# Retention scores in half-height tiles and an undecayed state in one PSUM bank, ahead of two expert MLPs

## The chip, the cores and the metric

One core of a Trainium2 chip runs the whole program. The metric is device time in microseconds (us) from the start to the end of one execution. The core's engines run side by side and meet at semaphores: PE (TensorE, matrix products into PSUM), ACT (ScalarE), DVE (VectorE), POOL (GpSimd) and SP (which issues DMAs). Each engine executes its own list of instructions in order.

## The reference, cut to what matters

```python
# q, k, v: (2 batches, 8 heads, 768 tokens, 64)
gamma = 1.0 - 2.0 ** (-5.0 - np.arange(H))
state = np.zeros((B, H, D, D))
for t in range(S):
    state = gamma * state + np.einsum('bhd,bhe->bhde', k[:, :, t], v[:, :, t])
    y[:, :, t] = scale * np.einsum('bhd,bhde->bhe', q[:, :, t], state)
x = y.transpose(0, 2, 1, 3).reshape(1536, 512)
# then a top-1 mixture of 8 experts (512 -> 1024 -> 512, relu), and
# relu(x @ w_in) ** 2 @ w_out with 512 -> 2048 -> 512
```

Only the first part, the retention, is touched by the change. Every head has its own decay gamma.

## The kernel before, in words

The 1536 tokens are 12 chunks of 128 (six per batch, `NC = 6`). The recurrence is done by chunks. With keys scaled by a falling and queries by a rising power of gamma, the output of a chunk is a masked product inside the chunk (scores, then scores times values) plus the queries times the state that the earlier chunks left. Products of this part are in f32, and PE records two MATMULs for each of them.

Eight heads of 64 lie as four pairs (`NP = 4`) of 128 rows. The functions for chunk i are:

- `khat`, `qhat` (L351, L355): scale K and Q on POOL, 128x512 each. `ktrans`, `qtrans` (L364, L372) transpose them on PE and copy them out of PSUM on ACT.
- `ktrans` (L364) writes the transposed keys into `kpads`, where each head has 128 rows and the other head's 64 rows are zeros set once at the start (L301 to L304). Two ACT copies of 64x512 do that.
- `scores` (L390): for each of eight heads one product of the padded keys (128 rows) with the pair's queries (L396), then two masked copies on DVE (L397).
- `outer` (L402): keys times values of a pair, 128x128, of which only the two diagonal 64x64 blocks belong to the state (L410). DVE adds the former state (L414; ACT copies instead in a batch's first chunk, L416), and POOL multiplies with `g128` (L418), which holds gamma to the 128th on the diagonal blocks and zeros elsewhere. The result `tf` serves `attend` of the next chunk.
- `attend` (L421): queries times `tf` (L430, four full products), then scores times values (L433, eight products of 64 output rows, two heads side by side in the halves of the columns), all into one bank.
- `halve`, `gate`, `probs`, `weigh`, `natural`, `count`, `rank`, `spread`, `enter` (L437 to L525) split the output into two f16 parts (`xlo` on DVE), compute the router, and build the table of tokens by expert.

The order is written out by hand (`manual_schedule`). The loop at L573 does for i = 0 to 10:

```python
attend(i); enter(i - 1); halve(i); scores(i + 1); gate(i); natural(i)
probs(i); count(i); outer(i + 1); weigh(i); ktrans(i + 2); qtrans(...)
qhat(...); rank(i); spread(i); khat(i + 3)
```

From i = 3 on (`L - PRE`) each iteration also splits half a block of expert weights: the high part on ACT after `halve`, the low part (`w1lo` or `w2lo`, L149) on DVE at the end of the iteration. `outer` returns at once for a batch's last chunk, so iteration 4 has no `outer`. Loads of K, Q and V run four chunks ahead on SP's queue. After the loop come the experts (to about 246 us) and the dense MLP.

Of the kernel before, what the change touches and what calls it, by code (L numbers as in the profile page):

```python
# [9 lines left out]
F32 = mybir.dt.float32  # L10
F16 = mybir.dt.float16
I32 = mybir.dt.int32
AF = mybir.ActivationFunctionType
ALU = mybir.AluOpType
# [5 lines left out]
P = 128  # L20
# [7 lines left out]
def layout_consts(B, H, S, D, E, cap, widths):  # L28

    gamma = 1.0 - 2.0 ** (-5.0 - np.arange(H, dtype=np.float64))  # L30
    t = np.arange(P, dtype=np.float64)
    cols = {}
    cols["ident"] = np.eye(P)

    tq = (2 * t[:, None, None] + np.arange(2)[None, None, :]) % P
    cols["gk"] = gamma[None, :] ** ((P - 1) - t[:, None]) * 256.0
    cols["gq"] = (gamma[None, :, None] ** (tq - (P - 1)) * 4.0).reshape(P, -1)
    cols["mask"] = (t[:, None] <= t[None, :]).astype(np.float64)
    cols["tail"] = np.zeros((P, 0))
    cols["w2e"] = np.tile(2.0 ** -np.arange(E), (P, 1))  # L40
    n_tile = B * S // P
    cols["tok"] = t[:, None] + P * np.arange(n_tile)[None, :]
    cols["tok1"] = cols["tok"] + 1
    cols["wide"] = np.tile(np.array(widths), (P, 1))
    arr = np.concatenate([cols[c] for c in cols], axis=1).astype(np.float32)
    where, o = {}, 0
    for c in cols:
# [13 lines left out]
def kernel(  # L61
# [19 lines left out]
    PE, ACT, DVE, POOL = nc.tensor, nc.scalar, nc.vector, nc.gpsimd  # L81
    B, H, S, D = q.shape
# [11 lines left out]
    NP = H // 2  # L94
    NC = S // P
# [19 lines left out]
    def C(n, i=None):  # L115
        o, w = where[n]
        src, o = (c32t, o - last) if o >= last else (c32, o)
        return src[:, o:o + w] if i is None else src[:, o + i:o + i + 1]
# [171 lines left out]
    sb = actx.enter_context(tc.tile_pool(name="sb", bufs=2))  # L290
    ld = actx.enter_context(tc.tile_pool(name="ld", bufs=5))
    ps = ctx.enter_context(tc.tile_pool(name="ps", bufs=1, space=PSUM))
# [5 lines left out]
    table_up = sb.tile([P, 1], F32, name="table_up", bufs=1)  # L298
    DVE.memset(table_up, 0.0)
    ACT.activation(out=table_up, in_=table_up, func=AF.Copy)  # L300
    kpads = []  # L301
    for i in range(2):
        kpads.append(sb.tile([P, NP, 2, P], F32, name=f"kpad{i}", bufs=1))
        POOL.memset(kpads[i], 0.0)  # L304
    g128 = sb.tile([P, NP, P], F32, name="g128", bufs=1)
    POOL.memset(g128, 0.0)
    for h in range(H):
        r = slice(h % 2 * D, (h % 2 + 1) * D)
        POOL.memset(g128[r, h // 2, r], float((1.0 - 2.0 ** (-5.0 - h)) ** P))
    wg = sb.tile([P, KD, E], F32, name="wg", bufs=1)  # L310
    wghi = sb.tile([P, KD, E], F16, name="wghi", bufs=1)
    wglo = sb.tile([P, KD, E], F16, name="wglo", bufs=1)
# [21 lines left out]
    Q, K, V = {}, {}, {}  # L334
# [11 lines left out]
                store[i] = ld.tile([P, H, D], F32, name=nm, tag=nm)  # L346
                nc.sync.dma_start(store[i], src[b, :, c * P:(c + 1) * P, :].rearrange("h t d -> t h d"))

    QH, KH, QT, SC, A = {}, {}, {}, {}, {}

    def khat(i, eng=POOL):  # L351
        KH[i] = sb.tile([P, H, D], F32, name="kh", tag="kh", bufs=3)
        eng.tensor_tensor(KH[i], K.pop(i), C("gk").unsqueeze(2).to_broadcast([P, H, D]), op=ALU.mult)

    def qhat(u, r, eng=POOL):  # L355
        if 2 * u >= NT:
            return
        QH[u, r] = sb.tile([P, H, D], F32, name="qh", tag="qh")
        eng.tensor_tensor(QH[u, r], Q[u][:, :, r, :],
                           C("gq").rearrange("p (h r) -> p h r", r=2)[:, :, r:r + 1].to_broadcast([P, H, D]), op=ALU.mult)  # L360
        if r == 1:
            Q.pop(u)

    def ktrans(i):  # L364
        tk = ps.tile([P, NP, P], F32, name="tk", tag="tk")
        for p in range(NP):
            PE.transpose(tk[:, p, :], KH[i][:, 2 * p:2 * p + 2, :].rearrange("t h d -> t (h d)"), C("ident"))
        for j in range(2):
            r = slice(j * D, (j + 1) * D)
            ACT.activation(out=kpads[i % 2][r, :, j, :], in_=tk[r], func=AF.Copy)  # L370

    def qtrans(u, r, tag="tq", eng=ACT):  # L372
        if 2 * u >= NT:
# [13 lines left out]
    def queries(i):  # L387
        return QT[i // 2][:, :, i % 2].rearrange("p n i r -> p n (i r)")

    def scores(i):  # L390
        A[i] = sb.tile([P, H, P], F32, name="A", tag="A")
        for u in range(2):
            sc = ps.tile([P, H // 2, P], F32, name="sc", tag=f"sc{u}")
            for h in range(u * H // 2, (u + 1) * H // 2):
                p, j = divmod(h, 2)
                PE.matmul(sc[:, h % (H // 2), :], lhsT=kpads[i % 2][:, p, j, :], rhs=queries(i)[:, p, :], start=True, stop=True)  # L396
            DVE.tensor_tensor(A[i][:, u * H // 2:(u + 1) * H // 2, :], sc, C("mask").unsqueeze(1).to_broadcast([P, H // 2, P]), op=ALU.mult)  # L397

    TF, XO = {}, {}
    XT = {}  # L400

    def outer(i):  # L402

        b, c = divmod(i, NC)
        if c == NC - 1:
            return
        pp = ps.tile([P, NP, P], F32, name="pp", tag="pp")
        kh = KH[i]
        for p in range(NP):
            PE.matmul(pp[:, p, :], lhsT=kh[:, 2 * p:2 * p + 2, :].rearrange("t h d -> t (h d)"),  # L410
                      rhs=V[i][:, 2 * p:2 * p + 2, :].rearrange("t h d -> t (h d)"), start=True, stop=True)
        t0 = sb.tile([P, NP, P], F32, name="t0", tag="t0")
        if c:
            DVE.tensor_tensor(t0, pp, TF[i], op=ALU.add)  # L414
        else:
            ACT.activation(out=t0, in_=pp, func=AF.Copy)  # L416
        tf = sb.tile([P, NP, P], F32, name="tf", tag="tf")
        POOL.tensor_tensor(tf, t0, g128, op=ALU.mult)  # L418
        TF[i + 1] = tf

    def attend(i):  # L421
        b, c = divmod(i, NC)
        xo = ps.tile([P, NP, P], F32, name="xo", tag="xo")
        qt = queries(i)
        a = A.pop(i)
        vv = V[i]

        if c:
            for p in range(NP):
                PE.matmul(xo[:, p, :], lhsT=TF[i][:, p, :], rhs=qt[:, p, :], start=(p == 0), stop=False, skip_group_check=True)  # L430
        for p in range(NP):
            for j in range(2):
                PE.matmul(xo[j * D:(j + 1) * D, p, :], lhsT=vv[:, 2 * p + j, :], rhs=a[:, 2 * p + j, :],  # L433
                          start=(c == 0 and p == 0), stop=(p == NP - 1), skip_group_check=True)
        XO[i] = xo

# [196 lines left out]
    for s_ in range(2):  # L633
        for kk in range(KD):
            for g, (off, n) in zip(g0, blocks(0)):
                n = min(n, widths[0] - off)
                PE.matmul(xb[s_][kk // 2][:, kk % 2, off:off + n], lhsT=g[0:n, s_ * DM + kk * P:s_ * DM + (kk + 1) * P],
                          rhs=C16("ident")[0:n, 0:n], start=False, stop=False, skip_group_check=True)
# [598 lines left out]
```

## Time and profile before

| | us |
|---|---|
| median of 3 runs (range) | 498.01 (497.55 to 499.4) |
| the profiled execution: its own time | 498.74 |
| its span in the profile | 497.0 |
| PE busy in the span | 473.5 (95%) |
| DVE busy | 333.0 (67%) |
| ACT busy | 272.2 (55%) |
| POOL busy | 102.8 (21%) |
| mean granted TensorE clock, share of full | 0.994 |

The profiled execution took 1.7 us more than its span: that much lies around the instructions. PE is the busiest engine over the whole program, but the three parts of the program (retention to about 92 us, experts to about 246 us, dense MLP to the end) need to be read apart. A matmul's record lasts longer than its turn, because matmuls overlap in the array: starts and sums of rows tell more than the mean length of one.

### The profile page before, as it was taken

To read this page: it belongs to the slowest core of one execution; us is meant where nothing else is said; L and a number is where in the kernel's file an instruction comes from. 1 tells how busy PE (TensorE), PEld (TensorE's weight loads), DVE (VectorE), ACT (ScalarE), POOL (GpSimd) and SP (SyncE) were. 2 spreads that over 40 slices of the span, in tenths; PEclk is the share of its full clock that TensorE was granted. 3 is DMA by queue.
4 is the path that set the end of the run, shared out by engine and by line. 5 is a ranking of instruction groups with operands and counts; after the bars stand their busy time and mean duration, and the time that the engine had idled before them with its cause. 6 is when DMAs were issued, how large, how long until landed. Compare 5 with 4: busy or idle time off the path is not lost.

```text
span 497.0 us, 9864 instructions
## 1 busy us (share of the span) xinstructions
PE 473.5 (95%) x4069; PEld 363.0 (73%) x4069; DVE 333.0 (67%) x573; ACT 272.2 (55%) x396; POOL 102.8 (21%) x120
## 2 busy tenths in 40 slices
PE   7999999888989999999999999999999999999991
PEld 4898899888989999899944444444458884447881
DVE  3778999897968889787789998406773114675110
ACT  3567675676665767672356655519882007884000
POOL 4755564291032431400000000011000110000100
PEclk9999999999999999999999999999999999999997
DMA  9998894599698898896452200011000100000100
GB/s 207 253 287 238 236 312 136 159 332 338 130 335 227 280 363 277 258 355 228 152 184 90 87 0 1 0 44 43 1 1 1 44 22 21 1 0 1 44 21 29
DMA packets 56120, 71.30 MB, mean 143 GB/s; under 512 B 30705, under 2 KB 37233, under 8 KB 55042
## 3 DMA queue, kind: packets, MB, share of 16 engines
q1 hardware_dynamic: 53410, 63.77, 42.0%
q0 software_dynamic: 2512, 6.73, 4.1%
q8 instruction: 34, 0.56, 0.5%
q14 instruction: 20, 0.16, 0.1%
q10 hardware_dynamic: 144, 0.08, 0.1%
HBM read 63.73 MB, written 6.84 MB: 142 GB/s over the span
## 4 chain that ended last, share of the span: by engine, by line
PE 77%; DMA 8%; DVE 5%; issue 3%; POOL 3%; ACT 2%; SPq 0%; POOLq 0%; ACTq 0%; DVEq 0%
PE w L1078 14%; PE zp L905 8%; PE zp L904 8%; PE zp L906 8%; DMA rawi<-in_moe_w_in_dram 4%; PE sc L396 4%; PE yp L728 3%; PE op L929 3%; PE op L930 3%; PE op L928 3%; PE yp L729 3%; PE yp L727 3%; PE hp L711 3%; PE hp L713 3%; PE hp L712 3%
## 5 line engine op out<-in xcount | busy, mean ns | idle before, releaser
L905 PE MATMUL zp<-ylo,winhi 128*128 128x512 f16 x192 | 72.8, 379 | 0.0
L904 PE MATMUL zp<-yhi,winhi 128*128 128x512 f16 x192 | 72.8, 379 | 0.0
L906 PE MATMUL zp<-yhi,winlo 128*128 128x512 f16 x192 | 72.8, 379 | 0.0
L728 PE MATMUL yp<-hl,w2hi 128*128 128x232 f16 (+5 forms) x256 | 65.4, 255 | 3.4 <-DVE hl L717 3.4
L919 POOL DMA_INDIRECT out_dram<-ob,tid x12 | 11.8, 982 | 264.6 <-DVE ob L1099 124.6
L727 PE MATMUL yp<-hh,w2hi 128*128 128x232 f16 (+5 forms) x256 | 65.4, 255 | 0.0
L729 PE MATMUL yp<-hh,w2lo 128*128 128x232 f16 (+5 forms) x256 | 65.4, 255 | 0.0
L1078 PE MATMUL w<-WH,AH 128*128 128x256 f16 x224 | 61.0, 273 | 0.5 <-ACT ob L1093 0.5
L1078 PE MATMUL w<-WH,AL 128*128 128x256 f16 x224 | 61.1, 273 | 0.0
L1078 PE MATMUL w<-WL,AH 128*128 128x256 f16 x224 | 61.0, 273 | 0.0
L711 PE MATMUL hp<-xg,w1hi 128*128 128x192 f16 (+5 forms) x224 | 57.0, 255 | 0.0
L713 PE MATMUL hp<-xg,w1lo 128*128 128x192 f16 (+5 forms) x224 | 57.0, 254 | 0.0
L712 PE MATMUL hp<-xg,w1hi 128*128 128x192 f16 (+5 forms) x224 | 57.0, 254 | 0.0
L1078 PEld LDWEIGHTS <-AH 128*128 128x128 f16 x448 | 43.8, 98 | 6.3 <-issue 0.9
L149 DVE SCALAR_TENSOR_TENSOR w2lo<-raw,w2hi 128x1024 f16<-128x1024 f32 x32 | 40.6, 1270 | 7.7 <-ACT w2hi L146 7.6
L1046 DVE TENSOR_TENSOR AL<-x,AH 128x768 f16<-128x768 f32 (+1 forms) x32 | 34.8, 1087 | 14.4 <-ACT AH L1044 14.4
L149 DVE SCALAR_TENSOR_TENSOR w1lo<-raw,w1hi 128x1024 f16<-128x1024 f32 x32 | 42.0, 1321 | 0.5 <-ACT w1hi L146 0.5
L146 ACT ACTIVATE w2hi<-raw 128x1024 f16<-128x1024 f32 x32 | 33.5, 1051 | 3.3 <-DMA raw<-in_moe_w_dram 3.1
L906 PEld LDWEIGHTS <-winlo 128*128 128x128 f16 x192 | 18.8, 98 | 22.5
L905 PEld LDWEIGHTS <-winhi 128*128 128x128 f16 x192 | 18.8, 98 | 22.5 <-DVE ylo L734 0.2
L904 PEld LDWEIGHTS <-winhi 128*128 128x128 f16 x192 | 18.8, 98 | 22.5
L146 ACT ACTIVATE w1hi<-raw 128x1024 f16<-128x1024 f32 x32 | 32.8, 1049 | 2.8 <-DMA raw<-in_moe_w_dram 2.8
(186 smaller groups left out, 1056.9 us busy)
## 6 DMA issues: line engine op xcount, KB each, us to landing
raw<-in_moe_w_dram SPq DMA_DIRECT2D x32, 1024.0 KB, 7.9
rawi<-in_moe_w_in_dram SPq DMA_DIRECT2D x8, 1024.0 KB, 9.5
rawo<-in_moe_w_out_dram SPq DMA_DIRECT2D x8, 1024.0 KB, 5.0
k<-in_k_dram SPq DMA_DIRECT2D x12, 256.0 KB, 4.5
q<-in_q_dram SPq DMA_DIRECT2D x6, 512.0 KB, 5.2
v<-in_v_dram SPq DMA_DIRECT2D x12, 256.0 KB, 5.3
xd<-row SPq DMA_DIRECT2D x12, 256.0 KB, 2.9
xd<-zrow SPq DMA_DIRECT2D x2, 256.0 KB, 5.9
```

What stands on the lines that cost most here:

```text
L146: ACT.activation(out=hi, in_=raw, func=AF.Copy, scale=WS)
L149: DVE.scalar_tensor_tensor(out=lo, in0=raw, scalar=WS, in1=hi, op0=ALU.mult, op1=ALU.subtract)
L711: PE.matmul(o, lhsT=w1h[:, kk, c], rhs=xh[kk], start=(kk == 0), stop=False)
L712: PE.matmul(o, lhsT=w1h[:, kk, c], rhs=xl[kk], start=False, stop=False)
L713: PE.matmul(o, lhsT=w1l[:, kk, c], rhs=xh[kk], start=False, stop=(kk == KD - 1))
L727: PE.matmul(o, lhsT=w2h[:, kk, c], rhs=hh[:, kk, :], start=(kk == 0), stop=False)
L728: PE.matmul(o, lhsT=w2h[:, kk, c], rhs=hl[:, kk, :], start=False, stop=False)
L729: PE.matmul(o, lhsT=w2l[:, kk, c], rhs=hh[:, kk, :], start=False, stop=(kk == KF - 1))
L904: PE.matmul(zp, lhsT=winhi[:, kk, c], rhs=yhi[kk // 2][:, kk % 2, cc], start=(kk == 0), stop=False)
L905: PE.matmul(zp, lhsT=winhi[:, kk, c], rhs=ylo[kk // 2][:, kk % 2, cc], start=False, stop=False)
L906: PE.matmul(zp, lhsT=winlo[:, kk, c], rhs=yhi[kk // 2][:, kk % 2, cc], start=False, stop=(kk == KD - 1))
L1078: PE.matmul(o, lhsT=a[:, s, kk, c], rhs=b[:, kk, w, :], start=(start and n == 1), stop=(stop and n == end), skip_group_check=True)
```

## The change

Scores use the two heads of a pair as two half-height products: head 0 has its keys and queries in rows 0 to 63, head 1 in rows 64 to 127, and they write to two different banks. The padded keys go, with one of two ACT copies. `outer` computes only the two diagonal 64x64 blocks, as eight products of 64 columns, and adds them up in a bank that is kept for the whole batch; no decay is applied, because the powers of gamma for keys and queries are now counted from the middle of the sequence and not from each chunk. ACT copies 128x256 out of that bank for `attend`. The sum on DVE, the product with `g128` on POOL and `g128` itself go. `attend` uses the state as eight products of 64x64 blocks on the diagonal of the array. The constants grow from 152 to 224 columns.

```diff
-    cols["gk"] = gamma[None, :] ** ((P - 1) - t[:, None]) * 256.0
-    cols["gq"] = (gamma[None, :, None] ** (tq - (P - 1)) * 4.0).reshape(P, -1)
+    cols["gk"] = (gamma ** (S // 2 - tk) * 256.0).reshape(P, -1)
+    cols["gq"] = (gamma[None, None, :, None] ** (tq - S // 2) * 4.0).reshape(P, -1)
...
-    kpads = []
-    for i in range(2):
-        kpads.append(sb.tile([P, NP, 2, P], F32, name=f"kpad{i}", bufs=1))
-        POOL.memset(kpads[i], 0.0)
-    g128 = sb.tile([P, NP, P], F32, name="g128", bufs=1)
...
-        for j in range(2):
-            r = slice(j * D, (j + 1) * D)
-            ACT.activation(out=kpads[i % 2][r, :, j, :], in_=tk[r], func=AF.Copy)
+        KT[i] = sb.tile([P, NP, P], F32, name="kt", tag="kt")
+        ACT.activation(out=KT[i], in_=tk, func=AF.Copy)
...
-                PE.matmul(sc[:, h % (H // 2), :], lhsT=kpads[i % 2][:, p, j, :], rhs=queries(i)[:, p, :], start=True, stop=True)
+        for p in range(NP):
+            for j, r in enumerate(HALF):
+                PE.matmul(sc[j][:, p, :], lhsT=kt[r, p, :], rhs=queries(i)[r, p, :], start=True, stop=True)
...
-            PE.matmul(pp[:, p, :], lhsT=kh[:, 2 * p:2 * p + 2, :].rearrange("t h d -> t (h d)"),
-                      rhs=V[i][:, 2 * p:2 * p + 2, :].rearrange("t h d -> t (h d)"), start=True, stop=True)
-        if c:
-            DVE.tensor_tensor(t0, pp, TF[i], op=ALU.add)
-        else:
-            ACT.activation(out=t0, in_=pp, func=AF.Copy)
-        POOL.tensor_tensor(tf, t0, g128, op=ALU.mult)
+            for j, r in enumerate(HALF):
+                PE.matmul(PP[0][r, p, :], lhsT=KH[i][:, 2 * p + j, :], rhs=V[i][:, 2 * p + j, :], start=(c == 0 and p == 0),
+                          stop=(p == NP - 1), skip_group_check=True)
+        TF[i + 1] = sb.tile([P, NP, D], F32, name="tf", tag="tf")
+        ACT.activation(out=TF[i + 1], in_=PP[0], func=AF.Copy)
...
-                PE.matmul(xo[:, p, :], lhsT=TF[i][:, p, :], rhs=qt[:, p, :], start=(p == 0), stop=False, skip_group_check=True)
+                for r in HALF:
+                    PE.matmul(xo[r, p, :], lhsT=TF[i][r, p, :], rhs=qt[r, p, :], start=(p == 0), stop=False, skip_group_check=True)
```

On POOL, one iteration of the loop before (`R` and `ot` are `count`'s small sums, `tf` the decayed state, `qh` and `kh` the scaled queries and keys):

```order
L500 TENSOR_TENSOR R_118<-R_117,OH 128x8
L504 TENSOR_TENSOR ot<-OH,c32t 128x8
L418 TENSOR_TENSOR tf<-t_1011,g_103 128x512
L359 TENSOR_TENSOR qh<-q,c_92 128x512
L353 TENSOR_TENSOR kh<-k,c_92 128x512
```

and the same iteration of the change:

```order
L490 TENSOR_TENSOR R_104<-R_103,OH 128x8
L494 TENSOR_TENSOR ot<-OH,c32t 128x8
L352 TENSOR_TENSOR qh<-q,c_92 128x512
L346 TENSOR_TENSOR kh<-k,c_92 128x512
```

The state's product is gone, and the two scalings move up by one place. On ACT, one iteration of the loop before, from `probs` on:

```order
L469 ACTIVATE pr,sm<-lg,nb 128x8
L370 ACTIVATE kpad_99<-tk 64x4x128 x2
L385 ACTIVATE qt<-tq 128x512
L441 ACTIVATE xhi<-xo 128x512
L146 ACTIVATE w2hi<-raw 128x1024
L488 ACTIVATE row<-xn 128x1024
```

and the same iteration of the change:

```order
L459 ACTIVATE pr,sm<-lg,nb 128x8
L408 ACTIVATE tf<-pp 128x256
L362 ACTIVATE kt<-tk 128x512
L377 ACTIVATE qt<-tq 128x512
L431 ACTIVATE xhi<-xo 128x512
L147 ACTIVATE w2hi<-raw 128x1024
L478 ACTIVATE row<-xn 128x1024
```

The copy of the state stands ahead of the one key copy that is left.

## Rows read from the trace of the kernel before

**Rows 1.** Busy time by stretch: retention loop, experts (us, engines with record counts, clock, DMA share).

```profile
core 0: us, PE busy (x) PEld busy (x) DVE busy (x) ACT busy (x) POOL busy (x), PEclk, DMA share, GB/s
9.00:92.00 83.00, 79.55 (x961) 74.23 (x962) 68.57 (x197) 52.30 (x96) 45.55 (x62) 1.00 0.88 236
92.00:246.00 154.00, 147.86 (x1645) 145.06 (x1645) 128.97 (x182) 96.23 (x125) 40.10 (x30) 1.00 0.82 268
```

**Rows 2.** Chain that ended last, in the loop (start us, length us, what).

```profile
19.62 1.00 PE xo L430 x8
...
32.96 1.00 PE xo L430 x8
...
59.81 1.00 PE xo L430 x8
60.81 1.02 PE xo L433 x16
...
61.99 1.89 PE sc L396 x16
...
64.78 0.95 PE pp L410 x8
...
80.03 1.00 PE xo L430 x8
...
84.86 0.95 PE xo L430 x8
```

**Rows 3.** Timeline of PE, 40 to 53 us (start us, length us, engine, line, what).

```profile
46.09 1.14 PE L430 MATMUL xo<-qt,tf 128*128 128x128 f32 x8
47.15 1.09 PE L433 MATMUL xo<-A,v 128*64 128x128 f32 x16
48.18 0.23 PE L524 MATMUL tb<-ot,pl 128*128 128x8 f16 x3
...
50.88 1.11 PE L410 MATMUL pp<-v,kh 128*128 128x128 f32 x8
51.83 0.60 PE L367 MATMUL tk<-c,kh 128*128 128x128 f32 x4
```

**Rows 4.** Timeline of DVE, iteration 4, which has no `outer`.

```profile
42.91 0.17 DVE L525 TENSOR_TENSOR table<-tb,table 128x24 f32<-128x24 f32 x1
...
45.38 0.15 DVE L462 TENSOR_SCALAR nb<-mx 128x1 f32<-128x1 f32 x1
46.02 0.15 DVE L475 TENSOR_SCALAR g<-sm 128x1 f32<-128x1 f32 x1 [0.48 <-ACT pr L469]
...
47.05 2.06 DVE L149 SCALAR_TENSOR_TENSOR w1lo<-raw,w1hi 128x1024 f16<-128x1024 f32 x1
49.03 0.17 DVE L525 TENSOR_TENSOR table<-tb,table 128x24 f32<-128x24 f32 x1
```

**Rows 5.** Timeline of POOL, the same iteration 4.

```profile
45.65 0.20 POOL L500 TENSOR_TENSOR R<-R,OH 128x8 f16<-128x8 f16 x1 [1.76 <-DVE nb L462]
...
45.96 1.05 POOL L359 TENSOR_TENSOR qh<-q,c 128x512 f32<-128x512 f32 x1
46.97 1.06 POOL L353 TENSOR_TENSOR kh<-k,c 128x512 f32<-128x512 f32 x1
```

**Rows 6.** Timeline of DVE, iteration 7, which has the sum of the state.

```profile
63.09 0.17 DVE L525 TENSOR_TENSOR table<-tb,table 128x24 f32<-128x24 f32 x1
...
65.83 0.69 DVE L414 TENSOR_TENSOR t<-pp,tf 128x512 f32<-128x512 f32 x1
...
69.90 0.17 DVE L525 TENSOR_TENSOR table<-tb,table 128x24 f32<-128x24 f32 x1
```

**Rows 7.** Timeline of POOL, the same iteration 7.

```profile
66.61 1.27 POOL L418 TENSOR_TENSOR tf<-t,g 128x512 f32<-128x512 f32 x1 [0.42 <-DVE g L475]
```

**Rows 8.** Groups by line and shape, up to 130 us (count, busy us, mean ns, idle before).

```profile
L416 ACT ACTIVATE t<-pp 128x512 f32<-128x512 f32 x2 | 1.2, 598 | 0.0
```

**Rows 9.** Who waited for whom, 92 to 250 us (us in total, times, longest us).

```profile
DVE single L164 <- DMA rawi<-in_moe_w_in_dram: 8.3, 5, 2.6
...
PE yp L728 <- DVE hl L717: 3.4, 3, 1.7
```

More of the change, by code (lines that the diff above doesn't have):

```diff
@@ L33, in layout_consts @@
     cols["ident"] = np.eye(P)
-    tq = (2 * t[:, None, None] + np.arange(2)[None, None, :]) % P
-    cols["gk"] = gamma[None, :] ** ((P - 1) - t[:, None]) * 256.0
-    cols["gq"] = (gamma[None, :, None] ** (tq - (P - 1)) * 4.0).reshape(P, -1)
+    tk = t[:, None, None] + P * np.arange(S // P)[None, :, None]
+    tq = 2 * (t[:, None, None, None] + P * np.arange(S // (2 * P))[None, :, None, None]) + np.arange(2)
+    cols["gk"] = (gamma ** (S // 2 - tk) * 256.0).reshape(P, -1)
+    cols["gq"] = (gamma[None, None, :, None] ** (tq - S // 2) * 4.0).reshape(P, -1)
     cols["mask"] = (t[:, None] <= t[None, :]).astype(np.float64)
@@ L300 @@
     ACT.activation(out=table_up, in_=table_up, func=AF.Copy)
-    kpads = []
-    for i in range(2):
-        kpads.append(sb.tile([P, NP, 2, P], F32, name=f"kpad{i}", bufs=1))
-        POOL.memset(kpads[i], 0.0)
-    g128 = sb.tile([P, NP, P], F32, name="g128", bufs=1)
[L306 to L309, printed above, removed]
     wg = sb.tile([P, KD, E], F32, name="wg", bufs=1)
@@ L347, in load @@
                 nc.sync.dma_start(store[i], src[b, :, c * P:(c + 1) * P, :].rearrange("h t d -> t h d"))
-    QH, KH, QT, SC, A = {}, {}, {}, {}, {}
+    QH, KH, KT, QT, A = {}, {}, {}, {}, {}
+    HALF = [slice(j * D, (j + 1) * D) for j in range(2)]
     def khat(i, eng=POOL):
         KH[i] = sb.tile([P, H, D], F32, name="kh", tag="kh", bufs=3)
-        eng.tensor_tensor(KH[i], K.pop(i), C("gk").unsqueeze(2).to_broadcast([P, H, D]), op=ALU.mult)
+        eng.tensor_tensor(KH[i], K.pop(i), C("gk")[:, i % NC * H:(i % NC + 1) * H].unsqueeze(2).to_broadcast([P, H, D]), op=ALU.mult)
     def qhat(u, r, eng=POOL):
@@ L359, in qhat @@
         eng.tensor_tensor(QH[u, r], Q[u][:, :, r, :],
-                           C("gq").rearrange("p (h r) -> p h r", r=2)[:, :, r:r + 1].to_broadcast([P, H, D]), op=ALU.mult)
+                           C("gq").rearrange("p (c h r) -> p c h r", h=H, r=2)[:, u % (NC // 2), :, r:r + 1].to_broadcast([P, H, D]), op=ALU.mult)
         if r == 1:
@@ L390, in scores @@
     def scores(i):
[L391 to L395, printed above, removed]
-                PE.matmul(sc[:, h % (H // 2), :], lhsT=kpads[i % 2][:, p, j, :], rhs=queries(i)[:, p, :], start=True, stop=True)
-            DVE.tensor_tensor(A[i][:, u * H // 2:(u + 1) * H // 2, :], sc, C("mask").unsqueeze(1).to_broadcast([P, H // 2, P]), op=ALU.mult)
+        A[i] = sb.tile([P, 2, NP, P], F32, name="A", tag="A")
+        sc = [ps.tile([P, NP, P], F32, name="sc", tag=f"sc{j}") for j in range(2)]
+        kt = KT.pop(i)
+        for p in range(NP):
+            for j, r in enumerate(HALF):
+                PE.matmul(sc[j][:, p, :], lhsT=kt[r, p, :], rhs=queries(i)[r, p, :], start=True, stop=True)
+        for j in range(2):
+            DVE.tensor_tensor(A[i][:, j], sc[j], C("mask").unsqueeze(1).to_broadcast([P, NP, P]), op=ALU.mult)
     TF, XO = {}, {}
     XT = {}
+    PP = []
     def outer(i):
@@ L406, in outer @@
             return
-        pp = ps.tile([P, NP, P], F32, name="pp", tag="pp")
-        kh = KH[i]
+        if c == 0:
+            PP[:] = [ps.tile([P, NP, D], F32, name="pp", tag="pp")]
         for p in range(NP):
-            PE.matmul(pp[:, p, :], lhsT=kh[:, 2 * p:2 * p + 2, :].rearrange("t h d -> t (h d)"),
-                      rhs=V[i][:, 2 * p:2 * p + 2, :].rearrange("t h d -> t (h d)"), start=True, stop=True)
-        t0 = sb.tile([P, NP, P], F32, name="t0", tag="t0")
-        if c:
-            DVE.tensor_tensor(t0, pp, TF[i], op=ALU.add)
-        else:
-            ACT.activation(out=t0, in_=pp, func=AF.Copy)
-        tf = sb.tile([P, NP, P], F32, name="tf", tag="tf")
-        POOL.tensor_tensor(tf, t0, g128, op=ALU.mult)
-        TF[i + 1] = tf
+            for j, r in enumerate(HALF):
[3 more added lines that the diff above has]
+        ACT.activation(out=TF[i + 1], in_=PP[0], func=AF.Copy)
     def attend(i):
@@ L429, in attend @@
             for p in range(NP):
-                PE.matmul(xo[:, p, :], lhsT=TF[i][:, p, :], rhs=qt[:, p, :], start=(p == 0), stop=False, skip_group_check=True)
+                for r in HALF:
+                    PE.matmul(xo[r, p, :], lhsT=TF[i][r, p, :], rhs=qt[r, p, :], start=(p == 0), stop=False, skip_group_check=True)
         for p in range(NP):
-            for j in range(2):
-                PE.matmul(xo[j * D:(j + 1) * D, p, :], lhsT=vv[:, 2 * p + j, :], rhs=a[:, 2 * p + j, :],
+            for j, r in enumerate(HALF):
+                PE.matmul(xo[r, p, :], lhsT=vv[:, 2 * p + j, :], rhs=a[:, j, p, :],
                           start=(c == 0 and p == 0), stop=(p == NP - 1), skip_group_check=True)
```

## The prediction

> **What bounds the kernel now.** I first cut the time into stretches. In the retention loop (9 to 92 us) PE is busy 79.55 of 83.00 us at a granted clock of 1.00, which is the 2.4 GHz level; ACT has 30 us of slack there and POOL 37 [rows 1]. So a shorter list for PE should pay here, until another engine's list becomes the longer one. DVE, with 68.57 us, is the nearest. In the experts PE is busy 147.86 of 154.00 us [rows 1].
>
> Then the chain. An iteration without a weight split lasts (32.96 - 19.62) / 2 = 6.67 us, and iterations 3 to 9 last (80.03 - 32.96) / 7 = 6.72 us [rows 2]. The chain lies on PE nearly all the way: 1.00 us for the state's products, 1.02 for scores times values, 1.89 for the scores, 0.95 for the outer products [rows 2]. The change touches three of these four.
>
> Then the pair of rows that prices half tiles. Scores and scores times values both show 16 records with 128 moving columns, but the 16 full ones take 1.89 us and the 16 on half the columns 1.02 [rows 2]. Two halves beside each other cost about what one full record costs. From 8 full records (1.00) to 16 (1.89), one more costs 0.89 / 8 = 0.111 us.
>
> Last, what stands behind PE. DVE's own turn, from one `table` sum to the next, is 6.81 us where the state's sum (0.69) is in it [rows 6], and 49.03 - 42.91 = 6.12 us in iteration 4, which has neither that sum nor POOL's decay [rows 4]. In that turn `nb` is followed by `R`, `qh` and `kh` on POOL (45.65 to 48.03), and `w1lo` takes 2.06 us: it starts with `kh` at 47.05 and ends 1.08 us after `kh` does [rows 4, 5]. I read that as DVE held until POOL is through.
>
> **The parts, on PE, for one iteration.** A change of tile has a price. From the first state product to the first half-column product are 47.15 - 46.09 = 1.06 us for 8 records, where 8 outer records take 51.83 - 50.88 = 0.95 up to the transposes, which need no change [rows 3]: 0.11 for the way in. The half-column products last 48.18 - 47.15 = 1.03 [rows 3]; 8 pairs at 0.111 are 0.89, which leaves 0.14 for the exposed first load and the way out.
>
> *Scores.* No row shows half-height tiles. At worst the halves don't overlap: 16 x 0.111 + 0.11 + 0.14 = 2.03 us. At best they pair as half columns do: 1.03 + 0.11 = 1.14. I take 1.14, because the half-column row is the nearest, the halves are separate rows of the array, and they write separate banks. Against 1.89: -0.75.
>
> *Outer products.* Eight pairs of half columns, as the trace has them, but with 64 moving columns. Upper bound: the price of 128 columns, 1.14. Lower bound: columns and loads are both half of a full tile's, so half of 0.89, plus 0.25: 0.70. I take 0.70, since those two numbers are all that is left to pay for; against 0.95: -0.25, with +0.19 as the other end.
>
> *State's products.* Twice as many on quarter tiles, two at a time: 0.89 as before, plus a way in and an exposed load that full tiles did not have. 1.00 becomes 1.1: +0.1. If the two diagonal blocks didn't overlap, 16 x 0.111 + 0.14 = 1.9: +0.9.
>
> Together -0.90 us per iteration, 5.8 in place of 6.67.
>
> **Other engines.** DVE loses 8 sums of 0.69 [rows 6]. POOL loses the decay (1.27) [rows 7] and the zeroing at the start, which lies before the first queries land. ACT loses one 64x512 copy and gains one of 128x256: the 128x512 copy took 0.598 [rows 8], so the new one costs at most that and the two nearly cancel; with 30 us of slack I cost it at nothing. It stands before the key copy, but the keys it delays are for scores a whole iteration later. The new state copy also has an iteration until `attend` reads it. PE's next sum in that bank waits for the copy of one iteration before, which is long done. The DMAs are the same but for 72 columns of constants; they run at 0.88 share in the loop [rows 1], with loads four chunks ahead, so they can follow a loop that is a tenth shorter.
>
> **Where the gain stops.** From iteration 3 on, DVE and POOL carry the weight split. With PE at 5.8, what is late next is `xlo`, which stands behind `w1lo` in DVE's list, and PE's router products wait for it. Every such iteration then has the list of iteration 4, so I take its 6.12 us as the turn.
>
> The sum, by stretch of the chain [rows 2]:
>
> - up to 19.62 (two scores, two outer products, no state): 2 x (0.75 + 0.25) = 2.0
> - iterations 1 and 2, PE's pace: 2 x 0.90 = 1.8
> - iterations 3 to 9, DVE's pace: 47.07 - 7 x 6.12 = 4.2
> - iteration 10 (80.03 to 84.86, scores alone): 0.7
>
> That is 8.7 us at the end of the loop. Behind it the list is unchanged, and every load there is issued when a split frees its buffer, so it moves with the rest. PE's waits there are small (3.4 us on `hl`, behind DVE's wait for `rawi`) [rows 9]. I take off 0.2 for a load that comes no earlier: 8.5 us. The profiled execution took 498.74, so 490.2; the median of the runs lies 0.7 below that execution (498.01), which would make 489.5, and I write **490.0 us**.
>
> **Rivals.**
>
> *The loads of half-height tiles come one after another (chance 0.10).* Then the scores keep 16 turns of 0.111 and pay the tile changes: 2.03 against 1.89, +0.14. The state's loads are half as wide and stay covered (+0.1); the outer products gain 0.25. PE's iteration stays at about 6.67, and only the few tenths by which DVE was late in some of iterations 3 to 9 come back: about -0.9 us, 497.8. Against it: the half-column loads are covered in pairs, or 16 records could not take 1.02 us; but those are 64 wide, and the scores' are 128 wide. The Trainium skill, "TensorE: Matmul & The Clock Gate", section "LDWEIGHTS (loading the stationary operand)", says that a load takes time by its columns and that fewer rows don't shorten it; if the two halves share one path, that is this rival. The trace shows no load with 64 rows, so no row decides it.
>
> *Half-height tiles run strictly one after another, and the kernel gets slower (0.09).* Scores 2.03 (+0.14) and state 1.9 (+0.9), outer products -0.25: +0.8 for each of ten iterations, less nothing, as PE stays the bound: 498.7 + 8 = 507. The point from which it decides: with a pair at y us, scores, state and outer change by 8y + 0.25 - 1.89, 8y + 0.25 - 1.00 and -0.25; that is zero at y = 0.165, half way from 0.111 (side by side) to 0.222 (in turn). For it: the state's blocks share a bank, which the scores' don't. Against it: the blocks lie in different partitions of that bank, as the half columns of L433 do, and those overlap.
>
> *The loop gains, the experts give back (0.05).* If their loads, at a DMA share of 0.82 [rows 1], set the pace there, a loop that ends 8.5 us earlier makes DVE wait longer for `rawi` (8.3 us now) and PE for `hl` [rows 9]. Half given back is 494.5. Against it: PE is busy 96% of that stretch.
>
> *PE decides to the end (0.04).* If without the decay POOL is through so early that `w1lo` runs uncovered, iterations 3 to 9 last 5.8 us: another 7 x 0.3 = 2.2, so 487.8.
>
> **The numbers.** My forecast has 0.68, with 487 to 494 as its own range (the bound of the outer products and the DVE turn from 5.8 to 6.5 us). To it come 0.10 at 497.8, 0.09 at 507, 0.05 at 494.5, 0.04 at 487.8, and 0.04 for a loss of a few us from a wait that I don't see. The range 487.0 to 498.5 leaves out the slower cases and little else. A measurement of this kernel can tell 0.5%, about 2.5 us, from no change. Faster than 495.5: forecast, 494.5 and 487.8, 0.76 with a little of the forecast's tail off. Within: 0.12. Slower: 0.12.
>
> **What would show it.** In the chain after: 16 score records in about 1.1 us, 16 outer records in about 0.7 and 16 state records in about 1.0 to 1.1; iterations 1 and 2 at 5.8 us; from iteration 3 about 6.1, with `xlo` and `w1lo` in the chain; the last `attend` at about 76 and not 85 us. Wrong would be: scores still near 1.9 (the first rival), state near 1.9 (the second), or a `hl` wait grown by several us (the third).

## The result and the profile after

The changed kernel took 492.18 us (median of 4 runs, 490.25 to 495.83), the kernel before 498.19 (4 runs beside them, 497.55 to 499.4): a ratio of 0.9893, interval 0.985 to 0.9936. The prediction was 490.0, with a range of 487.0 to 498.5, so sign and range held and the size did not: 8.5 us were forecast, 5 to 6 came (3.2 to 7.5 by the interval). A repeat beside 26 runs of the kernel before gave 0.989 (0.9849 to 0.993). The profiled execution is the slowest of the four: 495.83 us, span 494.0, mean granted clock 0.983. In the experiments the profiled executions of *state_only* and *warm_count* were disturbed; from them I use only what lies ahead of the experts.

The stretches that answer to [rows 1], with three shorter ones (the next to last column but one is the granted clock):

```profile
core 0: us, PE busy (x) PEld busy (x) DVE busy (x) ACT busy (x) POOL busy (x), PEclk, DMA share, GB/s
9.00:92.00 83.00, 75.71 (x1151) 65.63 (x1152) 59.16 (x200) 48.88 (x95) 29.40 (x52) 0.96 0.91 250
92.00:246.00 154.00, 148.45 (x1629) 144.16 (x1627) 128.54 (x173) 93.92 (x123) 42.86 (x30) 0.99 0.81 265
9.00:12.00 3.00, 2.55 (x19) 2.33 (x20) 0.45 (x1) 0.39 (x1) 1.04 (x1) 0.54 1.13 229
84.00:88.00 4.00, 4.00 (x52) 3.82 (x51) 2.16 (x14) 1.27 (x3) 0.36 (x2) 0.57 0.47 129
145.00:150.00 5.00, 4.20 (x25) 3.27 (x25) 5.00 (x7) 2.00 (x2) 1.39 (x1) 0.66 0.54 108
```

POOL lost 16 us of work in the loop, 12.7 of it the decay; the rest is mostly `kh`, which fell from 1.40 to 1.06 us on the mean. DVE lost 9.4: 5.5 are the sums, and 4.9 are `pl`, which takes 0.35 us on the mean where it took 0.76 (against them stands a little more of the experts' work, which now begins inside the stretch). That second gain my sum did not name. New is the clock: 0.54, 0.57 and 0.66 on the mean of three short stretches, and 0.50, the 1.2 GHz level, in the middle of each. The kernel before has 1.00 in both of the stretches of [rows 1]; only in their last 6 to 7 us are both kernels at 0.50.

The chain that answers to [rows 2], and how a score pair looks:

```profile
9.45 2.08 PE sc L388 x16
...
19.32 1.02 PE xo L420 x16
...
21.53 1.09 PE sc L388 x16
...
27.03 8.32 DMA q<-in_q_dram
...
55.20 0.61 PE pp L405 x16
...
75.10 1.02 PE xo L420 x16
...
79.50 1.02 PE xo L420 x16
```

Sixteen half-height score records take 1.09 us (1.89 before), sixteen outer records 0.61 (0.95), the state's sixteen 1.02 (1.00). Seen one by one, the records of chunk 2 are:

```profile
L388 PEld LDWEIGHTS sc<-qt,kt x16: 182/188/188, 21.5 to 22.2; 64*128 64x128 f32 x16
L388 PE MATMUL sc<-qt,kt x16: 272/272/373, 21.5 to 22.3; 64*128 64x128 f32 x16
```

The columns are min, median and max in ns, then the first and last start. Sixteen loads of 188 ns are 3.0 us of loading, begun within 0.7 us, one every 0.05 us; the kernel before begins a full-height one every 0.11 us (21.6 to 23.3). So the loads of the two halves run beside each other. The rule of the Trainium skill that my first rival rested on ("TensorE: Matmul & The Clock Gate", "LDWEIGHTS (loading the stationary operand)": time by columns, fewer rows don't shorten a load) agrees with the trace: 188 ns for one load of 64 rows, where a 128-row one took 192 in the kernel before. It does not follow that the loads queue.

So the array did what I said, and the loss lies around it. By the starts of the state's products, in [rows 2] and above (31.40 is the timeline's 31.33, plus the 0.07 us by which the chain's row starts later):

| stretch | forecast gain | measured |
|---|---|---|
| up to the first state | 2.0 | 19.62 - 19.32 = 0.3 |
| iterations 1 and 2 | 1.8 | 13.34 - 12.08 = 1.3 |
| iterations 3 to 9 | 4.2 | 47.07 - 43.70 = 3.4 |
| iteration 10 | 0.7 | 4.83 - 4.40 = 0.4 |
| end of the loop | 8.7 | 5.4 |
| first expert product | 8.7 | 91.70 - 88.61 = 3.1 |
| span | 8.5 | 497.0 - 494.0 = 3.0 |

This is the profile of the slowest of the four, beside a kernel before at a mean granted clock of 0.994. The changed kernel's time goes with its clock: over both rounds its two executions at 0.994 took 490.25 and 489.83 us, the three at 0.983 took 494.74 to 495.83. So the forecast is met where the clock hardly falls. No profile of such an execution is kept, and its stretches can't be read.

PE's timeline of iteration 2, for [rows 3], and of the wait that follows it in iteration 3 (in brackets: idle before, and what ended it):

```profile
26.28 1.09 PE L423 MATMUL xo<-A,v 128*64 128x128 f32 x16
27.31 0.23 PE L514 MATMUL tb<-ot,pl 128*128 128x8 f16 x3
27.47 1.16 PE L388 MATMUL sc<-qt,kt 64*128 64x128 f32 x16
...
28.60 0.17 PE L442 MATMUL lg<-wglo,xhi 128*128 128x8 f16 x1
28.86 0.18 PE L443 MATMUL lg<-wghi,xlo 128*128 128x8 f16 x1
...
37.53 0.66 PE L360 MATMUL tk<-c,kh 128*128 128x128 f32 x4 [1.11 <-POOL kh L346]
```

POOL's, at that wait:

```profile
35.42 1.05 POOL L352 TENSOR_TENSOR qh<-q,c 128x512 f32<-128x512 f32 x1 [4.29 <-DMA q<-in_q_dram]
```

Two waits are new. The third router product starts 0.26 us after the second, for it waits for `xlo`; in the kernel before these products follow each other every 0.03 us. And in iteration 3 POOL stands 4.29 us for a q load, PE behind it 1.11. DVE and ACT of iteration 7, for [rows 4, 6]:

```profile
63.72 2.06 DVE L150 SCALAR_TENSOR_TENSOR w2lo<-raw,w2hi 128x1024 f16<-128x1024 f32 x1
65.70 0.17 DVE L515 TENSOR_TENSOR table<-tb,table 128x24 f32<-128x24 f32 x1
65.80 0.68 DVE L432 SCALAR_TENSOR_TENSOR xlo<-xo,xhi 128x512 f16<-128x512 f32 x1
```

```profile
65.09 0.60 ACT L431 ACTIVATE xhi<-xo 128x512 f16<-128x512 f32 x1 [1.15 <-PE xo L423]
```

`xhi` is ready at 65.69 and `w2lo` is through at 65.78: there the way over ACT and the way over DVE's list end together.

Behind the loop (POOL, DVE, PE):

```profile
81.60 0.93 POOL L285 DMA_INDIRECT gx<-xd,gidx  x1 [0.30 <-DVE w2lo L150]
...
82.71 0.21 POOL L494 TENSOR_TENSOR ot<-OH,c32t 128x8 f16<-128x8 f16 x1
```

```profile
82.96 0.16 DVE L503 SCALAR_TENSOR_TENSOR junk<-OH,rk 128x8 f32<-128x8 f16 x1 [1.40 <-PE rk L501]
```

```profile
81.52 0.17 PE L501 MATMUL rk<-R,c 128*128 128x8 f16 x1
83.63 1.06 PE L531 MATMUL xb<-p,row 128*128 128x232 f16 x8 [1.95 <-DVE p L525]
```

PE waits 1.95 us where it waited 0.70, and the stretch from 84 to 88 us has a granted clock of 0.57. From the last scores times values (80.45 us, before 85.73) to the first expert product it takes 8.2 us in place of 6.0. In the experts the waits of [rows 9] became 9.2 us for `rawi` and 4.8 for `hl`:

```profile
DVE single L165 <- DMA rawi<-in_moe_w_in_dram: 9.2, 4, 4.8
PE yp L718 <- DVE hl L707: 4.8, 4, 2.1
```

### The profile page after: what moved, and what is told of

Read it like the earlier page. It is cut to its first block, busy times and chain, and to the rows that moved or that the text cites. A ratio compares the mean times of both kernels' runs of the same rounds, so it can differ in the third digit from the quotient of the medians.

```text
span 494.0 us, 10144 instructions
## 1 busy us (share of the span) xinstructions
PE 468.1 (95%) x4229; PEld 352.4 (71%) x4229; DVE 321.3 (65%) x565; ACT 265.3 (54%) x392; POOL 85.7 (17%) x99
## 4 chain that ended last, share of the span: by engine, by line
PE 70%; DMA 10%; DVE 10%; ACT 4%; issue 3%; POOL 1%; SPq 0%; ACTq 0%; POOLq 0%; DVEq 0%
PE w L1068 14%; PE zp L895 8%; PE zp L894 8%; PE zp L896 8%; DMA rawi<-in_moe_w_in_dram 5%; PE yp L718 3%; PE op L919 3%; PE op L920 3%; PE op L918 3%; PE yp L719 3%; DMA q<-in_q_dram 3%; PE yp L717 3%; DVE w1lo L150 3%; PE hp L701 2%; PE hp L703 2%
## 5 line engine op out<-in xcount | busy, mean ns | idle before, releaser
L150 DVE SCALAR_TENSOR_TENSOR w1lo<-raw,w1hi 128x1024 f16<-128x1024 f32 x32 | 40.4, 1271 | 0.3 <-ACT w1hi L147 0.3
```

Of the source, the lines that this page charges most:

```text
L150: DVE.scalar_tensor_tensor(out=lo, in0=raw, scalar=WS, in1=hi, op0=ALU.mult, op1=ALU.subtract)
```

## The experiments

**The change in two parts.** *scores_only* is the kernel before with half-height scores and plain keys alone; *state_only* is the kernel before with the undecayed state, the half-column outer products and the quarter tiles alone. *after_again* is the changed kernel. *clear_later* moves its two DMAs of zeros:

```diff
-        if i == 1:
+        if i == 6:
             clear()
...
```

> The kernel before with the half-height scores alone (one key copy, no padded keys); the decayed state stays as it was. Theory A (DVE's and POOL's turn bounds iterations 3 to 9): scores fall from 1.89 to 1.1 us, but DVE's turn with the state's sum stays at 6.7 to 6.8 us, so only the start and iterations 1, 2 and 10 gain: 2 to 3.5 us less than before, 494.5 to 496. Theory B (PE's list alone counts): 12 times 0.75 us, 8 us or more less than before, about 489 to 490.

> The kernel before with the undecayed state alone (diagonal outer products, state products on diagonal blocks, no sum on DVE, no decay on POOL); the scores keep their padded keys. Theory A: PE's iteration falls by about 0.35 us (outer 0.95 to 0.6, state unchanged) and stays the bound at 6.3 to 6.4 us, since DVE's turn is then 6.1: 3 to 4 us less than before, 494 to 495. Theory B expects the same from PE. If DVE's sum alone were what counted, iterations would fall to 6.1 and the time by 6 us.

> The changed kernel once more, unchanged. If the spread of its runs comes from stretches at the lower clock after PE gaps, runs with a mean granted clock of 0.994 lie near 490 us and runs with 0.983 near 495 to 496, and the stretches differ from profile to profile. If the spread had another cause, time and clock would not go together.

> The changed kernel with the two DMAs of zeros (512 KB) issued in iteration 6 in place of 1. If the third query load comes late because the DMA queues are full in the first 40 us, it lands about 2 us earlier, POOL's wait of 4.3 us shrinks, and iteration 3 falls from 7.25 to about 6.1 us: 1 us less than the changed kernel. Rival: that load is late because it is issued late, behind the wait for the row of iteration 1 on SP's queue; then the wait and iteration 3 stay.

Measured beside 26 runs of the kernel before (median 498.95): *scores_only* 0.9982 (0.9959 to 1.0005), *state_only* 0.9947 (0.9915 to 0.998), *after_again* 0.989 (0.9849 to 0.993), *clear_later* 0.990 (0.9852 to 0.9947). The chain of *scores_only*, then of *state_only*:

```profile
20.86 1.00 PE xo L427 x8
...
23.05 1.09 PE sc L392 x16
...
27.04 1.00 PE xo L427 x8
```

```profile
25.49 1.02 PE xo L424 x16
...
30.34 0.61 PE pp L409 x16
32.01 1.02 PE xo L424 x16
```

With the scores alone, iteration 1 falls from 6.67 to 27.04 - 20.86 = 6.18 us. With the state alone iterations last 32.01 - 25.49 = 6.52. Both fell short of what I expected: 0.9982 and 0.9947 of 498.95 are about 498 and 496.3 us, and not 494.5 to 496 and 494 to 495. Each part brings less than the two together (0.2%, 0.5%, 1.1%), but the intervals are too wide to say that the whole is more than the sum. The traces say it better. With the scores alone the later iterations go back to 6.5 to 6.8 us, with DVE's sum, `pl` and `w1lo` in the chain; iterations 5 and 6 together even took 16.03 us (12.20 in the changed kernel), with a granted clock of 0.50 from 58 to 61 us. With the state alone PE's own list still has the long scores. That part of the prediction stands: most of what the scores save is kept only once DVE and POOL are relieved.

In *clear_later* iteration 3 fell from 7.25 to 6.07 us, as expected: that wait was for bytes that stood ahead of the load. The time did not move. Iteration 7 took 0.42 us of the gain back (6.49 for 6.07). The rest went at the start of this execution, where the clock was at 0.50 from about 7.5 to 14.2 us and the first state's products began at 20.23 and not 19.25 us. So this run does not show that another load has to pay.

**Order in the loop.** *outer_first* puts the outer products between the scores and the router's products, *pool_early* puts `qhat` and `khat` ahead of `count` from i = 4 on, *both* does both, and *count_first* issues the gather after `count` in iteration 10.

```diff
         scores(i + 1)
+        if i < L - 1:
+            outer(i + 1)
         gate(i)
...
-        outer(i + 1)
```

```diff
         scores(i + 1)
+        if i >= 4:
+            if i < L - 1:
+                qhat(*turn(i + 1))
+            if i + 3 < NT:
+                khat(i + 3)
         gate(i)
...
```

> The changed kernel with the outer products issued before the router's products and not behind the transposes. Theory: the shorter scores no longer cover the 1.4 us from the end of scores times values over the halves (xhi, xlo) to the router, so PE waits about 0.25 us in each iteration; the outer products (0.6 us) cover that. Iterations 1 and 2 fall from 6.01 and 6.07 to about 5.75 us. From iteration 4 on DVE's and POOL's turn (6.05 us) stays, so the total gains only 0.5 to 1 us on the changed kernel. Rival (PE's chain through the halves alone bounds all iterations): all fall to 5.75, 2.5 to 3 us.

> The changed kernel with the scaling of queries and keys on POOL issued before the counts from iteration 4 on, so that w1lo no longer waits for it. Theory: w1lo falls from 2.07 to about 1.2 us, DVE's turn from 6.05 to 5.2, but PE's list with its wait for the halves, 6.0 us as in iterations 1 and 2, is then the bound: iterations 4 to 9 at about 6.0, no gain that can be measured. Rival (DVE's and POOL's turn alone bounds): they fall to 5.8 or less, 1.5 us or more.

> Both moves together. Theory (two turns of nearly the same length, each must be shortened): iterations 4 to 9 fall to about 5.75 us, in all 2 to 3 us less than the changed kernel, more than the sum of the two alone. If only one of the turns bounds, this kernel is no better than the better of the two.

> The changed kernel with POOL's count of iteration 10 issued before the gather of the first expert's rows. Theory: PE's gap of 1.95 us at the end of the loop (0.70 before the change) is the wait for that count, which stands behind the gather in POOL's list, and the gather waits for the last row to land. The gap falls to 0.5 to 0.9 us, 1 us off the time, a little more where the lower clock that follows the gap goes too. Rival: the products that need the gathered rows then wait instead, since the gather starts about 0.7 us later, and nothing is gained.

Measured beside 25 runs of the kernel before: *outer_first* 0.9866 (0.9816 to 0.9916), *pool_early* 0.9977 (0.994 to 1.0015), *both* 0.9997 (0.996 to 1.0034), *count_first* 1.0032 (0.9997 to 1.0067).

*outer_first* missed what I expected of it: iterations 1 and 2 grew from 6.0 to 6.3 us (its time can't be told from the changed kernel's). PE's timeline shows why:

```profile
26.35 0.17 PE L499 MATMUL rk<-OH,c 128*128 128x8 f16 x1 [0.48 <-ACT pr L459]
```

The wait for `xlo` is covered, but the router's products end later, the copy of `row` on ACT and `pr` behind it come later, and `rk`, which is written into the bank that `pr` reads, now waits for them. The cover only moved the wait.

*pool_early* puts a POOL product that needs a load ahead of a count that PE needs. In its chain:

```profile
45.13 3.03 DMA k<-in_k_dram
48.16 0.62 POOL kh L346
```

Iteration 5 then lasts 9.96 us and iteration 7, behind a q load, 7.13; iterations 8 and 9, free of such waits, keep 6.07 and 6.03. So neither `qh` nor `kh` sets the pace there, and putting them ahead costs most of the gain (0.9977 for 0.989). *both*, from which I expected 2 to 3 us, has both drawbacks: iterations of 6.3 to 6.4 us, and at 49.88 us PE waits 2.62 us for `ot`, which stands behind `qh` on POOL, and `qh` there behind its load. In *count_first* the wait ahead of the first expert's rows fell to 0.70 us, but the gather stood for the landing of row 10 and came late, which cost more:

```profile
80.65 3.10 DMA xd<-row
...
86.13 4.04 DMA gx<-xd,gidx
```

**The clock, the end of the loop, the turn.** *warm_start* puts nine more warming products into PE's idle stretches before the first scores. *count_dve* gives the two sums of `count` in iteration 10 to DVE. *rank_late* is *outer_first* with `rank`, `spread` and the low half of the split one step later, between the state's products and scores times values of the next chunk.

```diff
+    def fill(n):
+        for _ in range(n):
+            PE.matmul(wu, lhsT=warm[:, 0:P], rhs=warm, start=True, stop=True)
     ktrans(0)
+    fill(4)
...
     qtrans(0, 0, "tq", DVE)
+    fill(2)
...
     qtrans(0, 1, "sc1")
+    fill(3)
```

```diff
     def count(i):
+        eng = DVE if i == L - 1 else POOL
...
-            POOL.tensor_tensor(R[(i + 1) % 2], R[i % 2], oh, op=ALU.add)
+            eng.tensor_tensor(R[(i + 1) % 2], R[i % 2], oh, op=ALU.add)
...
```

```diff
-        attend(i)
+        attend(i, (lambda: late_rank(i - 1)) if i else None)
...
+    def late_rank(i):
+        rank(i)
+        spread(i)
+        if L - PRE <= i:
+            half_step(split_lo)
```

> The changed kernel with nine more warming products (the same 128x512 ones that stand at the start, into the same bank, their result unused) put into PE's three idle stretches before the first scores: four behind the first key transposes, two and three behind the two query transposes. Theory A (the clock at the start is given by PE's idle stretches before the first scores, 0.92 and 0.71 us in the changed kernel's profile): the granted clock stays at 1.00 from 9 to 15 us, the first 16 score records take about 1.1 us in place of 2.08, scores times values of the first chunk start near 12 and not 13.07 us, and the time is 1 to 1.5 us below the changed kernel's (ratio to before about 0.987). Theory B (half-height scores at the very start draw the lower clock whatever stands ahead of them): they take 2 us again, the granted clock is 0.50 there, and the fillers cost nothing or a few tenths.

> The changed kernel with the two small sums of count in iteration 10 (R and ot, 0.2 us each) given to DVE in place of POOL, where they stand behind the gather's two instructions. Theory A (the 1.95 us in which PE waits before the first products of the first expert's rows, where the kernel before waited 0.70, is rank waiting for R behind the gather, and that wait is what lowers the granted clock at 84.7): the wait falls to 0.7 to 0.9 us, the granted clock stays at 1.00 from 84 to 88 us, and 1.2 us by the wait and up to 1.7 by the clock come off, in all 1 to 3 us. Theory B (the wait is held by something else that comes as late, the split of w2 on DVE or row 10): the wait stays above 1.5 us and the time does not move.

> The changed kernel with the outer products between the scores and the router's products, where they cover the wait for xlo, and with rank, spread and the low half of the weight split put one step later, between the state's products and scores times values of the next chunk, so that PE no longer waits for R and pr in front of the state. Theory A (PE's own list with its one wait for xlo sets the 6.07 us everywhere): iterations 1 and 2 fall to about 5.75 and so do iterations 4 to 9; 2 to 3 us come off. Theory B, the prediction's (from iteration 3 on DVE's turn is the longer one): iterations 1 and 2 fall to about 5.75, iterations 4 to 9 stay at 6.0 to 6.2 with PE waiting for xlo behind w2lo, and at most 1 us comes off.

Measured beside 6 runs of the kernel before (median 500.18): *warm_start* 0.9867 (0.9814 to 0.9919), *count_dve* 0.9878 (0.9767 to 0.9989), *rank_late* 0.9878 (0.9792 to 0.9963). None can be told from the changed kernel. Their traces tell more. *warm_start* at its start, by stretch and on PE:

```profile
9.00:12.00 3.00, 2.90 (x41) 2.12 (x39) 1.20 (x2) 1.13 (x2) 1.04 (x1) 1.00 1.02 208
```

```profile
9.64 1.16 PE L388 MATMUL sc<-qt,kt 64*128 64x128 f32 x16
```

Theory A holds: with PE's idle stretches filled, the first half-height scores take 1.16 us at a granted clock of 1.00, where the changed kernel shows 2.08 at 0.50. The first scores times values start at 11.84 and not 13.07 us, the first state's products at 18.34 and not 19.25. At the end of the loop 0.7 us of this is left: iteration 1 lasts 6.27 us for 6.01, and iteration 3 still waits for its q load (6.91).

In *count_dve* the wait fell to 0.75 us and the granted clock stayed at 1.00 behind it, as theory A has it. But its mechanism is wrong. `rank` of iteration 10 reads the sum that the iteration before wrote; in *rank_late*, `p` follows on DVE while POOL has not yet begun that sum (`R`, at 82.87):

```profile
82.11 0.34 DVE L527 TENSOR_SCALAR p<-c,rnk,oh 128x232 f16<-128x232 f16 x1
```

What the trace of the changed kernel shows is narrower: `junk` has its input at 81.69 and starts at 82.96, 0.04 us after POOL's run of gather and two sums ends. And the short wait is not *count_dve*'s alone: in *after_again*, *warm_start* and *rank_late*, with POOL's list as it was, PE waits 0.70 to 0.79 us there, but then a second time, for the gather to land. In *after_again*:

```profile
87.32 0.96 PE L627 MATMUL xb<-c,gx 104*128 104x104 f16 x15 [1.29 <-DMA gx<-xd,gidx]
```

In the other two it is 0.57 and 0.72 us. From the last scores times values to the first expert product it takes 8.0, 6.8 and 6.9 us in these three, 8.2 in the changed kernel, 6.0 before and 6.0 in *count_dve*, whose POOL issues both gathers before `w2lo` begins on DVE (78.38 and 79.83 against 80.79 us; 80.15 and 81.60 against 80.35 in the changed kernel). So the place is the gather and what stands around it on POOL and DVE. All the kernels together say more. In six (before, *scores_only*, *state_only*, *pool_early*, *both*, *count_dve*) both gathers begin ahead of `w2lo`, and the stretch takes 5.97 to 6.02 us. In seven others (all the rest but *count_first*) the second or both begin later, and it takes 6.4 to 8.6. *warm_count*, below, with the sums of *count_dve* on DVE, is one of the seven (7.3). So it is the order that goes with the short stretch and not the edit of *count_dve*, whose sums stand behind the gathers anyway.

And DVE does hold POOL up there. A gather that begins just behind `w2lo` lasts 1.60 to 2.20 us (*after_again*, *warm_start*, *warm_count*, *outer_first*) in place of 0.93 to 1.15, and ends 0.8 to 1.0 us after `w2lo` does. In *after_again*:

```profile
81.18 1.22 DVE L150 SCALAR_TENSOR_TENSOR w2lo<-raw,w2hi 128x1024 f16<-128x1024 f32 x1
81.22 2.20 POOL L285 DMA_INDIRECT gx<-xd,gidx  x1 [5.13 <-DVE OH L450]
```

What holds `junk` is less clear. In the changed kernel and in *clear_later* the gather began 0.1 us ahead of its input, and it starts only after POOL's run; but in the four profiles just named it starts while the gather is still under way. What no run shows is why the first gather begins 1.4 to 2.7 us after its indices (`gidx`) in the seven and 0.3 to 0.6 us after them in the six; the landing of the row before it is a candidate that was not tested.

*rank_late*, on PE:

```profile
64.63 1.09 PE L425 MATMUL xo<-A,v 128*64 128x128 f32 x16
...
70.42 1.09 PE L425 MATMUL xo<-A,v 128*64 128x128 f32 x16
...
75.77 1.09 PE L425 MATMUL xo<-A,v 128*64 128x128 f32 x16
```

Iterations 8 and 9 last 5.79 and 5.35 us with the same work on DVE: the 6.12 us that I took for DVE's turn is no floor. But iterations 5 and 7 wait for q loads, and the end of the loop is where it was (80.56 us for the last scores times values; 80.45 in the changed kernel):

```profile
51.92 8.36 DMA q<-in_q_dram
60.35 1.05 POOL qh L352
```

**Both gains at once.** *warm_count* is *warm_start* and *count_dve* together.

> The fillers of warm_start and the sums of count_dve together, on the changed kernel: the candidate to beat it. Theory A (both gains are of the loop and its end, and pass through the experts): the first scores take 1.1 us at a granted clock of 1.00, PE waits 0.7 to 0.9 us before the first expert's rows, the first expert product starts at 85 to 86 us (88.61 in the changed kernel's profile, 91.70 in the kernel before), and the time is 1 to 3 us below the changed kernel's, ratio to before 0.983 to 0.988. Theory B (the experts take back what comes before them: PE waits longer for hl, and with a half clock behind it): the first expert product starts as early, but from there to the last one lasts over 156 us (154.4 in the kernel before, 155.5 and 152.4 in two profiles of the changed one), and the ratio stays at 0.987 to 0.992.

Measured beside 11 runs of the kernel before (median 498.72): 0.989 (0.9842 to 0.9939), the changed kernel's own ratio. The first expert product starts at 86.80 us, 1.8 us earlier than in the changed kernel, and nothing of it is seen in the time. That is theory B's number; but 1.8 us are 0.36%, and the interval reaches into theory A's range, so a gain of that size could hide in it. What the experts take back is read from the other profiles. In the order of their first expert product, with PE's waits for `hl` between 92 and 250 us and the time from that product to the end of the span:

| | first expert product | waits for `hl` | to the end |
|---|---|---|---|
| before | 91.70 | 3.4 | 405.3 |
| after_again | 89.24 | 3.2 | 402.7 |
| outer_first | 88.97 | 4.6 | 407.9 |
| after | 88.61 | 4.8 | 405.4 |
| rank_late | 87.43 | 3.5 | 405.1 |
| count_dve | 86.62 | 5.4 | 404.6 |
| warm_start | 86.50 | 7.2 | 410.7 |

The earliest two wait longest, though not in strict order; DVE's waits for `rawi` go from 8.3 us (before) to 12.1 and 11.0 in them. But the time to the end does not follow: *count_dve* starts as early as *warm_start* and takes no longer than the kernel before, and *outer_first*, which starts later than the changed kernel, takes 2.5 us more than it. So an early start can be taken back, as this execution of *warm_start* does with all of it; that it must be is not shown.

## Why the prediction was right, and where its sum failed

**Half-height tiles side by side: right.** 1.09 us for the scores (forecast 1.14), 0.61 for the outer products with about 0.1 for the way in (0.70), 1.02 for the state (1.1). Both rivals that rested on the array fall. The state copy on ACT took 374 ns, under the bound of [rows 8].

**"Together -0.90 us per iteration, 5.8": too much.** The three terms held, but 26.28 - 20.27 is 6.01 us and the next iteration 6.07. PE's list had a wait that the long scores had hidden: from the last product of scores times values over `xhi` (0.60) and `xlo` (0.69) to the router, 28.86 - 27.31 = 1.55 us, while `tb` and the short scores fill 1.25. The 0.26 us seen at the router is what is missing between 5.8 and 6.07. I costed the scores and did not ask what they covered. *outer_first* covers this wait and meets the next behind it: row, `pr`, `rk`.

**The start, 2.0: failed, 0.3 came.** I priced two chunks of scores and outer products at full clock. The first of them ran at half (2.08 us), and the k load came 0.3 us later (the first key transposes start at 5.40 and not 5.07 us). *warm_start* shows the clock's share: 1.2 us at the first scores times values, 0.9 at the first state. From 16.45 to 18.55 us the chain also lies on ACT, with `row` and the new state copy (`tf`, 0.27 us) in it; I had costed that copy at nothing.

**From iteration 3 on 6.12 a turn: right in size, half right in reason.** Iterations 4, 7, 8 and 9 last 6.02, 6.07, 6.13 and 6.03 us, and the chain does go over `w1lo`, `table` and `xlo`. But iterations 1 and 2 have no split and the same pace; in the profile after, PE's own ring and DVE's end within 0.1 us of each other, and *rank_late*, with another order, has shorter turns. What cost 1.1 us more than forecast in iteration 3 was a load.

**"They can follow a loop that is a tenth shorter": failed.** The share was 0.88 on the mean of the loop; in iteration 3 it is the wait for q that decides (4.29 us on POOL). *clear_later* takes that wait away by moving other bytes, and in *rank_late* two of the later turns still end in one.

**The pass-on of 8.5: failed in part.** The list behind the loop is unchanged, but 2.2 us were lost in it, around the gather: as a wait of 1.95 us and a half clock in the profiled execution; in *after_again* 2.0 us, as a wait of 0.83 where there was one of 0.33 and a new one of 1.29. That the shorter last scores no longer cover the gather is argued and not shown. The third rival, to which I gave 0.05, did not decide here: from the first expert product on, the changed kernel took as long as the one before (405.4 and 405.3 us). One profile, that of *warm_start*, shows it in full.

**The clock: not in the sum.** I priced every stretch at full clock. The executions at 0.994 came out at my 490.0, the others later, by and large the later the lower their clock was. So it is a term that I put at nothing without a reason. That 490.0 was met at 0.994 may be luck in part, for in the profiled execution the loop's gain is 3.3 us short of 8.7, and not all of that is clock.

What stays open: why the first gather begins late, what holds `junk` behind it, and which of the clock's falls come in which execution.

## What to carry to other kernels

When an instruction gets shorter, ask first what ran behind it: its length may have been the cover of a chain on two other engines, and the gain ends where that chain does. Where a kernel's loads are busy nine tenths of a stretch on the mean, "the loads can follow" has to be shown load by load, for a faster loop meets the one that is latest. Part gains that each stand in a trace need not show in the time: here a first expert product that came another 2 us earlier could not be told from none, with a spread of several us from the clock and longer waits in the stage behind it.

## What the runs showed of the hardware that was not expected

- Two 64-row products with 128 columns each, in the two halves of the array and into two banks, cost one turn: 16 in 1.09 us, where 16 full ones took 1.89. Their loads, 188 ns each, run side by side.
- Half-height products behind idle stretches of PE ran at half speed at the start: 2.08 us for the first 16 in the changed kernel; with the stretches filled they took 1.16 at a granted clock of 1.00. It does not take half height. In *after_again* the clock fell at about 7.9 us, and the second four query transposes, of full height, took 1.12 us (0.65 before) ahead of any half-height product:

```profile
7.90 1.12 PE L372 MATMUL tq<-c,qh 128*128 128x128 f32 x4 [0.25 <-POOL qh L352]
```

  Before the first query transposes PE was idle 0.62 us in the kernel before and 0.67 in *state_only* (both stayed at 1.00), and 0.74 to 1.34 in those whose granted clock fell. But that does not sort all of them: in *scores_only* (0.64 us idle) eight query transposes took 2.02 us and the first 16 scores 2.08, at half speed, although the granted clock reads 1.00 there. So that column does not show every such stretch, and no run varies the idle time alone.
- Short operations of one of DVE and POOL can last as long as a big one of the other: POOL's `R` took 1.07 us beside `w2lo` in *count_first*, DVE's `OH` 1.06 us beside `kh` in iteration 3 of the changed kernel; with nothing big beside them they take 0.20 and 0.23.
- In the kernel before, a wait of PE of 1.71 us at 149.50, in the middle of the experts, left the granted clock at 1.00. In the changed one a wait of 2 us there, with PE busy 2.76 of the 5.00 us up to 145, was followed by 0.50, seen here in the length of the products:

```profile
143.48 0.27 PE L717 MATMUL yp<-hh,w2hi 128*128 128x240 f16 x1
145.80 0.36 PE L718 MATMUL yp<-hl,w2hi 128*128 128x240 f16 x1 [2.06 <-DVE hl L707]
145.96 0.40 PE L719 MATMUL yp<-hh,w2lo 128*128 128x240 f16 x1
```
